# One layer (linear attention and a gated feed-forward) on one core: normalised tiles transposed in pairs, buffers resized, load waits moved, work re-ordered

## The chip, the cores and the metric

The kernel runs on one core of a Trainium2 chip. A core has a matmul engine (TensorE: PE in the profile, its weight loads PEld), a vector engine (VectorE: DVE), a scalar engine (ScalarE: ACT), a general engine (GpSimd: POOL), and a queue engine (SyncE: SP) that issues transfers; each runs its own stream of instructions in order, and they meet by semaphores. The metric is the device time of one execution in microseconds (us), as the median of the runs.

## The reference

Batch 1, 2048 rows, width 448, 16 heads of 28, feed-forward width 1792, all bf16:

```python
qkv = layernorm(x) @ wqkv                                   # q, k, v: 16 heads of 28
pq, pk = q @ w_phi[h], k @ w_phi[h]                         # per head
phi_q = concat(softmax(pq), softmax(-pq))                   # 56 features per head
phi_k = concat(softmax(pk), softmax(-pk))
kv, z = einsum("sf,sd->fd", phi_k, v), sum_s(phi_k)         # over all 2048 rows
o = (phi_q @ kv) / (phi_q @ z + 1e-6)
h = x + o @ wo
h2 = h + (sigmoid(g) * u) @ w_down                          # g, u = layernorm(h) @ w_gate, @ w_up
```

## The kernel before

**Tiles.** The 2048 rows are 16 tiles of 128 (NT). The feed-forward runs in five chunks of 2, 4, 4, 4 and 2 tiles (CH). Width 448 is padded to four blocks of 128 columns in the transposed arrays (the blocks overlap, and a matmul reads only the rows that are its own).

**First the weights.** The q and k weights are transposed (WT, copies WTc at L460/L463), centred, and multiplied by w_phi (fold, copies W2 at L483/L486), so that a projection gives the features' logits at once. v's weights are centred (Wvc).

**Keys.** For each tile: projection of k and v (kp, vp), two exponentials of plus and minus the logits on ACT (L599), a sum per head on DVE (ss, L612), its reciprocal (rs, L615), the scaling phi (L619, on POOL or DVE), and kv (L632), which adds the tile to one running product. When tile 15 is in, kvz (L696, DVE) masks and copies that product; nothing of the attention's output can start before it.

**Queries.** Projections qp, exponentials (eqp, eqm, L654), sums of the halves (hs on POOL, L668; sq on DVE, L671), reciprocals rq (L673, L675), the scaling em (L681, POOL or DVE), and a transpose by DMA into eqT (eT, L689; tiles 0 to 3 one by one, the others in pairs). Scaled features lie in a ring of NEQ buffers. Some scalings on DVE and on POOL are kept from running side by side: each waits for the last one of the other engine in the order (L127 to L134).

**Output of the attention.** num (numerator and denominator, L705), rd and o (division, L713 and L715, into o_pad), the transpose oT (tiles 0 and 1 by matmul and copy, oP L723 and oT L729; the others by DMA in pairs, L736), the output projection (wo_, for tiles 0 and 1 on top of x at L744; for the others a pair of tiles as two matmul streams on the upper and lower 64 rows of the array, `pair` and `half`, L510 to L522). Each pair has two halves of 4 and 3 passes; the second adds to the banks of the first.

**Second normalisation.** h (sum, L769), statistics (L772, L774), rs2 by a power on POOL (ve2 L775, pow2 L777), nb (L788), and hn (L784 for tiles 0 and 1, else L790 on ACT or L792 on DVE) into a ring of NHN buffers. Then the transpose hT into hnT: tiles 0 and 1 by matmul and copy (hP L798, copies L804/L807), tiles 2 to 15 each by one DMA transpose on SP (L810). hnT is the same memory as xT, the transposed input that the projections read.

**Feed-forward.** For each chunk and pair of 128-wide blocks: gate and up products as two 64-row streams (gu, L514 through `half`), tanh on ACT (tg, L845; the sigmoid is (tanh(g/2)+1)/2), hh = (tanh+1)*u on DVE (L852), then per tile the down product (dn, L871), the sum with h on DVE (fin, L878), and the store (st, L880). In the last chunk the down products, copies and stores are split into 336 and 112 columns (a and b), and tile 15's last store is issued by ACT, all others by SP. Dummy matmuls (dm, L814) can be placed where PE would stand still.

**The order.** Every piece of work is a task with a number. PLAN (L30 to L72) is the order of all tasks, written out: the task's number, after a point the banks of PSUM that it takes, and "~" where it runs on its other engine. `emit` (L148) walks the list once, puts each task at the end of its engine's queue, and adds the waits that its inputs, its bank and its buffer need. Loads, transposes and stores have their own rings of semaphores; before one certain store SP waits for the whole ring of loads and transposes (L170 to L175): the store with eight left to go, the eleventh of 18.

Of the kernel before, what the change touches and what calls it, by code (L numbers as in the profile page):

```python
# [10 lines left out]
P = 128  # L11
# [19 lines left out]
8 16 17 11 9 14 43 10 1 0 23 24 25 26 27 28 29 30 31 32 33 34 35 44 36 37 38 39 40 41 42 52 56 50 51 46 3 18 4 19 45  # L31
6 55 47 48 57.7-7 58 59 60 61 661.0-0 70.0-0 71 67.1-1 118 2 15 12 13 64.2-2 73.3-3 68 20 119 65 74 22 72 69 66~ 75
120 21 165.4-4 167.5-5 62 63 662.0-0 91.6-6 92 94.7-7 95 88.0-0 89 97.1-1 98 121 93~ 7 122 123 124 5 90~ 96~ 166 99
168 112.2-2 113 127 125 114 115 128 126 169.3-3 171 173 175 79.4-4 170.6-6 172 174 193.0-1 176 177.5-7 178 194
76.2-2 180 179 182 80 183 116 129 117 130 184 131 186 187 189 136 190 138 134 132 135 137 133 139 191 81 195.3-6 181
188 185.4-4 196 204 197 198 205 206 199 211.5-7 192 229.0-1 212 85.6-6 140 141 142 200 77 78 201 207 86 216 215 87
208 149 202 223 222 82.3-3 230 213.2-5 203 209 218 83 219 220 225 145 226 147 143 146 148 150 144 227 151 152 153 84
214 217 224 234 231.6-7 210 100.3-3 101 232 233 235 103.2-2 104 247.0-5 221 102 240 241 109.6-6 248 105 251 252 236
160 237 238 243 158 244 161 254 255 154 156 159 155 157 245 249.1-3 110 106.2-2 107 228 108 250 111 259 253 242 258
265.0-2 239 266 270 269 319.1-6 320 246 256 162 163 261 262 272 327 328 276 277 322 321 329 273 257 263 283.5-7  # L40
267.0-6 284 164 287 288 274 279 330 280 290 323 281 331 291 324 268 301.1-2 260 302 335.3-5 264 271 295 278 294 305
306 292~ 325 332 326 334 333 663.0-0 285.0-6 336 286 303.1-7 275 312 289 313 338 282 293 304 353.0-2 297 298 299 345
314 337 344 296 307 515.7-7 354 421.3-5 300 362 356 363 355 308 315 309 316 310~ 317~ 311 318 422 455 519.6-6
461.1-1 370.0-2 456.4-4 346 347 339 364 462 348 340 463 457 341 458 349 357 342 350 54 53 49 352 358 365 359 366 343
351 371 464.1-1 459.4-4 423 430 424 465 460 520 521 516 517 537 543 372 431 522 373 380 379 404.1-3 387.5-6 518 388
389 469.4-4 360 367 361 368~ 544 538 369 545 539 470 546 540 405 547.0-0 541.2-2 466.7-7 471 374 381 390 407 548 396
406 542~ 664.5-5 665.5-5 701.4-5 702.0-2 703 704 705 707 413 414 397 467 468 382 375 706 476.1-1 473.7-7 708 477 474
478 475 709.4-5 710.0-2 711 712 717.1-3 718.6-7 719 720 391 398 376 383 713 715 714 723 721 472 479 523.4-5 524 384
377 385 378 392 399 400 393 716 722 725.0-2 726.1-3 727 728 729 549 557 731 550 724 525.4-5 526 551 732 558 559 565
730 573 733.6-7 734.1-3 735 736 394 401 402 395 408 560 552 553 554 561 566 562 386 403 737 738 567 568 741.0-2  # L50
742.4-5 743 744 739 555 563 569 574 740 575 747 570 745 571 748 576 415 746 556 564 438.6-7 749.1-3 750.4-5 751 752
753 755 577 578 754 756 416 439 490.0-0 480.2-2 487.1-1 483.3-3 760.4-4 481 491 492 484 485 482 432 409 761 433 488
434 489 410 579 572 580 763.0-5 764.2-3 765 766 440 448 447 441 769 767 771.6-7 772.1-4 773 774 425 435 449 426 427
417 428 436 411 450 770 418 451 452 442 775 768 777 412~ 443 444 778 776 779.2-3 780.0-5 781 782 785 783 786 486 493
527.1-4 787.6-7 788.0-5 789 790 784 793 791 794 792 529.2-3 528 530 795.0-5 796.6-7 797 798 589 581 597 799 801 598
605 582 583 606 802 800 599 803.1-4 804.2-3 805 806 807 809 811.6-7 812.0-5 813 814 607 590 808 815 817 816 810 818
591 757.1-1 419 762 420 494.4-4 758 495 429 584 437 445 496 497.6-6 504.7-7 505 498 499 453 600 446 608 609 610 601
602 585 454 586 587 588 611 603 822.2-2 823 759 500 592 593 594 511.3-3 595 825.0-0 506 828.5-5 508.1-1 531.4-6
501.2-2 826 512 513 502 829 532 621 613 503 509 510 612 604 596 831.0-7 832.3-5 833 834 835 837 836 614 838 839.4-6
840.1-2 841 842 843 845 847.0-7 848.3-5 849 850 844 853 851 846 615 616 617 618 622 623 619~ 624 625 626 852 854  # L60
855.4-6 856.1-2 857 858 859 861 862 507 514 620 827 860 533.0-7 863.3-5 864.1-2 865 866 867 534 868 627~ 628 869 637
# [6 lines left out]
991.4-7 992.2-6 993 994 999.1-5 1000.0-3 1001 1002 995 997 998 996 1007.2-6 1008.4-7 1009 1010 1005 1003 1004 1006  # L68
1015.1-5 1016.0-3 1017 1018 1011 1012 1013 1019 1021 955.2-2 1022 956 1014 1023.6-6 958.0-0 961.3-3 1031.2-2 1020
962 1035.4-4 1036 1032 1033 959 964.7-7 965 1024 895 889 1034 892 898 957 963 960 966 1025 1026 1027.1-1 1037 1038  # L70
1028 1029 1030
"""  # L72


# [5 lines left out]
class _Graph:  # L80
# [67 lines left out]
    def emit(self, rings):  # L148

        nc = self.nc  # L150
        done = self.planned()
# [769 lines left out]
```

## Time and profile before

| | us |
|---|---|
| median of three runs | 206.84 (206.36, 206.84, 206.85) |
| the profiled execution | 206.24 |
| its span in the profile | 204.5 |

The span is the time from the first to the last event that the profile holds; 1.7 us of the execution lie around it. A row of a view has a start, a length, an engine, a line of the kernel and the operation; "[0.50 <-PE ps L514]" says that the engine stood still for 0.50 us before, and what ended that. The costliest group is the gate and up product, whose two streams are two groups of 490 matmuls each with 87.0 and 86.8 us that overlap each other; next comes the down product with 43.5 us.

### The profile page before, as it was taken

The numbers are of one execution on the slowest core, as the hardware profiler recorded it, in microseconds if no ns is written. First come the engines' busy times: TensorE is split into PE (matmuls) and PEld (weight loads), VectorE is DVE, ScalarE is ACT, GpSimd is POOL, SyncE is SP. The second block draws the span as 40 slices with busy tenths as digits, with TensorE's granted clock in tenths as the row PEclk, the third lists the DMA queues.
The fourth block names the chain that finished last, engine by engine and source line by source line (L and its number), as shares of the span: only waits on it lengthen the run. The fifth ranks groups of instructions, "written<-read, shape, count | busy, mean of one in ns | idle before, by whom it ended". The sixth has DMA issues, their size and how long they took to land.

```text
span 204.5 us, 5003 instructions
## 1 busy us (share of the span) xinstructions
PE 196.8 (96%) x2029; PEld 106.5 (52%) x2029; DVE 132.7 (65%) x306; ACT 96.0 (47%) x182; POOL 79.0 (39%) x141
## 2 busy tenths in 40 slices
PE   7899999999999998999999999999999999999993
PEld 3444454445377764555555544444544444886562
DVE  2999999898799979729574466465128345543033
ACT  3789999998983580423342042423002443551000
POOL 8569999768759865600830003003000300000000
PEclk9999999999999999999999999999999999999999
DMA  5999997059683955191155151013200004000014
GB/s 147 272 268 222 307 383 215 0 110 340 135 132 75 188 88 104 44 168 40 40 114 103 30 103 27 24 27 27 72 0 0 3 11 109 3 3 0 0 42 140
DMA packets 49751, 21.06 MB, mean 103 GB/s; under 512 B 40512, under 2 KB 48704, under 8 KB 49728
## 3 DMA queue, kind: packets, MB, share of 16 engines
q1 hardware_dynamic: 49584, 20.71, 44.6%
q8 instruction: 16, 0.26, 0.5%
q14 instruction: 7, 0.06, 0.1%
q10 hardware_dynamic: 144, 0.03, 0.1%
HBM read 9.20 MB, written 1.84 MB: 54 GB/s over the span
## 4 chain that ended last, share of the span: by engine, by line
PE 76%; ACT 7%; DVE 6%; POOL 5%; issue 2%; DMA 2%; SPq 1%; DVEq 0%; POOLq 0%; ACTq 0%
PE ps L514 51%; PE ps L871 21%; POOL hh L619 3%; ACT eq L654 2%; ACT hh L599 2%; DVE ssum L612 2%; DMA wphK<-in_A_w_phi_dram 2%; PE ps L705 1%; DVE hh L619 1%; POOL rs L543 1%; DVE x_sb L878 1%; PE ps L585 1%; SPq L358 1%; DVE sq L671 1%; PE ps L475 1%
## 5 line engine op out<-in xcount | busy, mean ns | idle before, releaser
L514 PE MATMUL ps<-xT,wg_sb 64*128 64x512 bf16 (+1 forms) x490 | 87.0, 333 | 1.1 <-DVE x_sb L878 0.7
L514 PE MATMUL ps<-xT,wu_sb 64*128 64x512 bf16 (+1 forms) x490 | 86.8, 333 | 0.0
L845 ACT ACTIVATE tg<-ps 128x512 f32<-128x512 f32 (+1 forms) x70 | 33.9, 511 | 76.8 <-PE ps L514 76.1
L852 DVE SCALAR_TENSOR_TENSOR hh<-tg,ps 128x512 bf16<-128x512 f32 (+1 forms) x70 | 38.2, 573 | 32.1 <-ACT tg L845 31.9
L514 PEld LDWEIGHTS ps<-xT,wg_sb 64*128 64x128 bf16 x490 | 45.6, 94 | 22.7 <-issue 1.9
L514 PEld LDWEIGHTS ps<-xT,wu_sb 64*128 64x128 bf16 x490 | 45.6, 94 | 15.2
L871 PE MATMUL ps<-wd_sb,hh 128*128 128x448 bf16 (+2 forms) x252 | 43.5, 332 | 0.0
L871 PEld LDWEIGHTS ps<-wd_sb,hh 128*128 128x128 bf16 x252 | 22.9, 98 | 19.3 <-issue 1.0
L878 DVE SCALAR_TENSOR_TENSOR x_sb<-ps,x_sb 128x448 bf16<-128x448 f32 (+2 forms) x18 | 10.0, 566 | 24.4 <-PE ps L871 24.4
L775 POOL TENSOR_SCALAR rs<-mv 128x1 f32<-128x1 f32 x14 | 2.7, 192 | 59.7 <-DVE mv L774 58.8
L619 POOL TENSOR_TENSOR hh<-hh,rsum 128x896 bf16<-128x896 bf16 x13 | 21.9, 1700 | 0.5 <-DVE rsum L615 0.5
L599 ACT ACTIVATE hh<-ps,rs 128x448 bf16<-128x448 f32 x32 | 18.7, 643 | 2.0 <-PE ps L585 1.1
L654 ACT ACTIVATE eq<-ps,rs 128x448 bf16<-128x448 f32 x32 | 18.1, 649 | 0.0
L612 DVE TENSOR_REDUCE ssum<-hh 128x32 f32<-128x896 bf16 x16 | 16.9, 1058 | 0.8 <-ACT hh L599 0.6
L668 POOL TENSOR_TENSOR halves<-eq 128x448 f32<-128x448 bf16 x14 | 13.4, 970 | 8.3 <-DVE sq L671 2.7
L514 PE MATMUL ps<-Wvc,xT 64*128 64x448 bf16 x112 | 13.2, 351 | 0.2
L681 POOL TENSOR_TENSOR eq<-eq,rq 128x448 bf16<-128x448 bf16 x14 | 13.0, 942 | 1.0 <-DVE eq L681 0.8
L514 PE MATMUL ps<-Wq,xT 64*128 64x448 bf16 x112 | 13.1, 351 | 0.1
L514 PE MATMUL ps<-Wk,xT 64*128 64x448 bf16 x98 | 11.5, 351 | 0.2
L514 PE MATMUL ps<-wo_sb,oT 64*128 64x448 bf16 x98 | 11.3, 350 | 0.1
L790 ACT ACTIVATE hn<-x_sb,nb,rs 128x512 bf16<-128x512 bf16 x10 | 7.8, 810 | 5.5 <-POOL nb L788 3.0
L715 DVE TENSOR_TENSOR o_pad<-ps,rden 128x448 bf16<-128x448 f32 x16 | 9.8, 620 | 0.2
(104 smaller groups left out, 186.4 us busy)
## 6 DMA issues: line engine op xcount, KB each, us to landing
wu_sb<-in_B_w_up_dram SPq DMA_DIRECT2D x2, 896.0 KB, 8.2
wg_sb<-in_B_w_gate_dram SPq DMA_DIRECT2D x2, 896.0 KB, 7.5
out_dram<-x_sb SPq DMA_DIRECT2D x14, 112.0 KB, 1.8
x_sb<-in_A_x_dram SPq DMA_DIRECT2D x3, 448.0 KB, 4.1
wd_sb<-in_B_w_down_dram SPq DMA_DIRECT2D x3, 448.0 KB, 4.6
hh<-in_A_wqkv_dram SPq DMA_DIRECT2D x4, 196.0 KB, 3.6
wo_sb<-in_A_wo_dram SPq DMA_DIRECT2D x2, 336.0 KB, 9.5
x_sb<-in_A_x_dram SPq DMA_DIRECT2D x2, 224.0 KB, 4.0
```

The source lines that it names most:

```text
L514: r = e.matmul(ap(), lhsT=st(blk, rows), rhs=mv(blk, rows), start=first and i == 0, stop=not first and i == 2, tile_position=(rows.start, 0))
L599: task((key, t), "act", 0.53, lambda e, t=t, s=s, i=i, b=kb: e.activation(signs(ek[:, s, :])[:, :, :, i, :], heads2(bank[b()][:, 0:D]), AC ...
L612: task(("ss", t), "dve", 1.0, lambda e, s=s: e.tensor_reduce(ssum[:, s, :], ek[:, s, :].rearrange("p (h d) -> p h d", d=DH), AX.X, ALU.add ...
L619: return e.tensor_tensor(phi[:, t % NPHI, :, 0:GP].rearrange("p k (a d) -> p k a d", d=DH), ek[:, s, :].rearrange("p (k a d) -> p k a d", ...
L654: task((key, t), "act", 0.53, lambda e, w=w, t=t, i=i, b=bk[j]: e.activation(signs4(eq[:, w, :, 0:GP])[:, :, :, i, :], heads2(bank[b()][:, ...
L668: task(("hs", t), "pool", 0.9, lambda e, w=w, half_=half_, by4=by4: e.tensor_tensor(half_, by4(eq[:, w, :, 0:GP])[:, :, :, 0:DH // 2], by4 ...
L681: return e.tensor_tensor(ap, ap, rq[:, w, :].rearrange("p (k h) -> p k h", h=2)[:, :, :, None].to_broadcast([P, NPAIR, 2, DH]), ALU.mult)
L715: task(("o", t), "dve", 0.56, lambda e, t=t, res=res: e.tensor_tensor(o_pad[:, t % 4, 64 * (t % 2):64 * (t % 2) + D].rearrange("p (h d) -> ...
L845: task(("tg", c, f_), "act", 0.51 if n == 4 else 0.3, lambda e, j=j, N=N, b=gb[i]: e.activation(tg[:, j % NSG, 0:N], bank[b()][:, 0:N], AC ...
L852: e.scalar_tensor_tensor(hhT[c % 2][:, f_, 0:N], tg[:, j % NSG, 0:N], 1.0, bank[b()][:, 0:N], op0=ALU.add, op1=ALU.mult), deps)
L871: r = e.matmul(bank[b][:, cols], lhsT=hhT[c % 2][:, f_, ts], rhs=wd_sb[:, f_, cols], start=(f_ == 0), stop=(f_ == FT - 1))
L878: e.scalar_tensor_tensor(X(t)[:, cols], bank[got(first)[0]][:, cols], 0.5, X(t)[:, cols], op0=ALU.mult, op1=ALU.add), [nm, ("hn", t)])
```

## The change

1. hnT is laid out tile by tile, `[p, tile, block, column]` where it was `[p, block, row]`, in the same memory. Tiles 2 to 15 are transposed in pairs: 7 DMA transposes of two tiles each, with a destination that is one stretch for the pair, where 14 single ones were. A pair waits for both normalised tiles, and for the projections of the input tiles over whose memory it writes: tile t lies over the columns of one block of input tiles 4(t mod 4) to 4(t mod 4)+3, for tiles 0 to 15 alike.
2. The gate and up products read their moving operand as `hnT[rows, t0:t0+n, blk, :]`: n runs of 128 columns, where it was one run of 128n.
3. NEQ is 12 (14), NHN is 4 (3).
4. SP's waits for the rings of loads and transposes stand before the first store that follows the issue of the last transpose (the ninth store in the new order).
5. PLAN is another order. On PE, seen from the order of each engine: the keys' projections of tile pair 0 have their halves next to each other; before the first gate product the query projections of pairs 3 to 6 stand earlier, among tile 0's and tile 1's output work; the output projections of tiles 2 and 3 and of 4 and 5 have their halves parted by the halves of query projection 7; three dummies where five stood; the last down products run in another order and the last one is tile 15's. On the other engines: tile 12's phi is POOL's (DVE's before); em.0, em.4 and em.5 are DVE's (em.5 and em.10 before), em.0 ahead of kvz; h.0, hn.5, hn.6 and hn.8 are DVE's (ACT's before), hn.11, hn.12 and hn.14 ACT's (DVE's before); one weight copy (WTc.1.0) is ACT's (DVE's before). On SP the weight loads of the feed-forward all stand ahead of the first feature transpose, and the last store is ACT's, of tile 15's narrow columns.

```diff
-    NEK, NPHI, NV, NEQ, NSG, NHN = 3, 3, 3, 14, 3, 3
+    NEK, NPHI, NV, NEQ, NSG, NHN = 3, 3, 3, 12, 3, 4
...
-        hnT = xT
+        hnT = xT[:].rearrange("p k s -> p (k s)").rearrange("p (t k s) -> p t k s", t=NT, k=4)
...
-            n_out = sum(t.kind == "out" for t in done)
+            n_tr, checked = sum(t.kind == "tr" for t in done), False
             for t in done:
-                if t.kind == "out" and nring.get("out", 0) == n_out - 8:
+                if t.kind == "out" and nring["in"] == rings["in"] and nring["tr"] == n_tr and not checked:
+                    checked = True
                     for k in ("in", "tr"):
                         for j in range(min(nring[k], rings[k])):
                             wait("sp", ring_sems[k][j], (k, j), 16 * ((nring[k] - 1 - j) // rings[k] + 1))
...
+        HT = {t: ("hT", t if t < 2 else t - t % 2) for t in range(NT)}
...
-            free = [opt(("hT", t - NHN))]
+            free = [opt(HT.get(t - NHN))]
...
-            read = [Q_OF[t], ("kp", t // 2, 1), ("vp", t // 2, 1)]
+            over = [4 * (i % 4) + j for i in ((t,) if t < 2 else (t - 1, t)) for j in (0, 2)]
+            read = [d for i in over for d in (Q_OF[i], ("kp", i // 2, 1), ("vp", i // 2, 1))]
...
-            else:
-                task(("hT", t), "sp", 1.25, lambda e, t=t: e.dma_start_transpose(
-                    out=hnT[:, :, TS(t)], in_=hn[:, t % NHN, :]), [("hn", t)] + read, lat=1.6 if t < 6 else 2.8, kind="tr", size=0.72)
+            elif t % 2:
+                task(("hT", t - 1), "sp", 1.25, lambda e, t=t: e.dma_start_transpose(
+                    out=hnT[:, t - 1:t + 1, :, :].rearrange("p t k s -> p (t k) s"),
+                    in_=hn[:, (t - 1) % NHN:(t - 1) % NHN + 2, :].rearrange("p t k -> p (t k)")),
+                    [("hn", t - 1), ("hn", t)] + read, lat=1.6 if t < 6 else 2.8, kind="tr", size=1.42)
...
-                    return (lambda: bank[b()][:, 0:N], lambda blk, rows: w[rows, blk, fs], lambda blk, rows: hnT[rows, blk, cs])
+                    return (lambda: bank[b()][:, 0:N], lambda blk, rows: w[rows, blk, fs], lambda blk, rows: hnT[rows, t0:t0 + n, blk, :])
...
-                             [nm + (i, 0)] if h else GU_W + [("hT", t) for t in range(t0, t0 + n)],
+                             [nm + (i, 0)] if h else GU_W + [HT[t] for t in range(t0, t0 + n)],
```

The copies of tiles 0 and 1 (L804, L807) write `hnT[:, t, :, :]` in place of `hnT[:, :, TS(t)]`. The numbers in PLAN are left out here: task numbers shift by the seven transposes that are gone, so its text differs throughout.

More of the change, by code (lines that the diff above doesn't have):

```diff
@@ L36 @@
[L36 to L45, printed above, removed]
@@ new lines @@
+932.0-2 933.3-7 934 935 938 936 937 939 940.1-6 941.4-5 942 943 944 946 945 947 960.0-2 961.3-7 962 963 968.1-6
+969.4-5 970 971 964 966 967 965 972 974 975 973 976.3-7 977.0-2 978 979 980 982 981 983 984.4-5 985.1-6 986 987 988
+990 991 989 992.3-7 993.0-2 994 995 1008.1-6 1009.4-5 1010 1011 998 996 997 999 1012 1013 1000.3-7 1001.0-2 1002
+1003 1006 1007 954.1-1 948.6-6 951.0-0 952 1004 949 1005 955 957.2-2 1016.0-0 958 1024.6-6 950 953 814 959 1014 1015
+1020.3-3 1021 1022 1023 888 1017 1018 1019 956 1025 1028.7-7 1026 1027 1029 1030 1031
```

74 lines of the change are left out of this document (38 added, 36 removed).

## The prediction

> **What bounds the kernel now.** First the head of the profile's page, then busy time by stage (columns: window, its length, busy time and instruction count of PE, PEld, DVE, ACT, POOL, then PEclk, DMA share, GB/s).
>
> ```profile
> span 204.5 us, 5003 instructions
> PE 196.8 (96%) x2029; PEld 106.5 (52%) x2029; DVE 132.7 (65%) x306; ACT 96.0 (47%) x182; POOL 79.0 (39%) x141
> ```
> ```profile
> 0.00:10.00 10.00, 7.57 (x55) 3.98 (x55) 5.97 (x25) 5.23 (x9) 7.21 (x26) 1.00 0.86 210
> 10.00:47.00 37.00, 36.43 (x430) 17.48 (x431) 34.97 (x76) 35.17 (x67) 30.23 (x32) 1.00 0.82 215
> 47.00:58.00 11.00, 10.24 (x109) 4.77 (x111) 9.61 (x27) 10.17 (x21) 9.28 (x15) 1.00 0.88 236
> 58.00:78.54 20.54, 19.68 (x301) 13.98 (x302) 18.34 (x49) 11.87 (x26) 14.31 (x27) 1.00 0.67 108
> 78.54:201.41 122.87, 122.86 (x1140) 66.25 (x1140) 63.50 (x131) 33.58 (x62) 17.99 (x44) 1.00 0.23 47
> 201.41:204.50 3.09, 0.00 (x0) 0.00 (x0) 0.30 (x2) 0.00 (x0) 0.00 (x0) 1.00 0.51 158
> ```
>
> TensorE's clock is granted in full everywhere, so no term below is a clock's. From 78.54 to 201.41 PE is busy 122.86 of 122.87 us: there only fewer or cheaper matmuls help, and the matmuls stay the same in number and size. From 10 to 58 DVE and ACT are nearly as full as PE, so the first 58 us are a balance of four engines in which PE's time is stretched by whichever is late. What is left is the gap before 78.54 (20.54 less 19.68 in that stage) and the 3.09 us after the last matmul. The chain of waits (start, length, what) names the joints:
>
> ```profile
> 57.98 1.71 PE ps L514 x28
> ...
> 75.20 2.67 PE ps L871 x14
> ...
> 78.54 23.98 PE ps L514 x224
> ...
> 185.33 15.39 PE ps L871 x98
> ...
> 200.75 0.69 DVE x_sb L878 x2
> 201.44 0.27 DVE x_sb L878
> ```
>
> The first gate product starts at 57.98 (G below), the second chunk's at 78.54, and the end is a copy and a store behind the last down product.
>
> **The change, part by part.**
>
> *Front, up to G.* The new order gives tile 12's K scaling to POOL, one weight copy to ACT, and em.0, em.4 and em.5 to DVE (before: em.5 alone of these). h.0 moves to DVE too, behind ve2.0, where it runs while POOL takes tile 0's power: 0. Rows of the timeline:
>
> ```profile
> 35.78 3.36 POOL L619 TENSOR_TENSOR hh<-hh,rsum 128x896 bf16<-128x896 bf16 x2
> ...
> 40.80 1.84 POOL L681 TENSOR_TENSOR eq<-eq,rq 128x448 bf16<-128x448 bf16 x2
> 42.60 1.70 POOL L619 TENSOR_TENSOR hh<-hh,rsum 128x896 bf16<-128x896 bf16 x1
> ```
> ```profile
> 39.45 1.09 DVE L619 TENSOR_TENSOR hh<-hh,rsum 128x896 bf16<-128x896 bf16 x1 [0.22 <-POOL rq L675]
> ...
> 44.43 2.09 DVE L619 TENSOR_TENSOR hh<-hh,rsum 128x896 bf16<-128x896 bf16 x2
> 47.02 0.64 DVE L696 TENSOR_TENSOR kvz<-ps,maskP 112x464 bf16<-112x464 f32 x1 [0.49 <-PE ps L632]
> ...
> 53.87 0.62 DVE L681 TENSOR_TENSOR eq<-eq,rq 128x448 bf16<-128x448 bf16 x1 [0.16 <-POOL eq L681]
> ...
> 55.55 0.26 DVE L713 RECIPROCAL rden<-ps 128x16 f32<-128x16 f32 x1 [0.93 <-PE ps L705]
> ```
>
> POOL is free of tile 11 at 39.13. From there it runs two small rq (0.2 each; DVE's 0.22 of waiting at 39.45 was for one), scaling 12 (1.70), one em (0.92) and scaling 13 (1.70): 43.8. DVE's sums come 1.09 earlier without scaling 12, so its last two scalings (2.09) start at 43.8 and end at 45.9 instead of 46.53: kvz could start 0.63 sooner. em.0 (0.62) now stands on DVE ahead of kvz, in a place where DVE waits 0.49 for PE: +0.13. em.4 and em.5 are both on DVE between the two tiles' statistics and their normalising, one more than before: +0.62, unless it falls into DVE's 0.93 us wait at 55.55. Tile 0's features are scaled last (45.9 + 0.62 = 46.5, where POOL had them at 42.6), so its numerator comes behind tile 1's by the length of a transpose, and four more projection parts are ordered ahead of it; these parts are work that PE did later before, so they cost G only as far as tile 0 waits for them. A freer DVE in the start stage gives perhaps 0.3. Sum: -0.63 + 0.13 + 0.62 - 0.3 = **-0.2**. Bounds: -1.4 (the extra em falls into the wait of 0.93 and tile 0 is not late, -0.8; and POOL, lighter by 0.92 for each em given away, brings tile 0's last scale another 0.6 forward) and +1.2 (no gain at the start, 0.62 in full, tile 0 later by its own 0.62 and 0.4 more). Two of five dummies go:
>
> ```profile
> L814 PE MATMUL ps<-warm 128*128 128x512 bf16 x5 | 2.0, 429 | 0.0
> ```
>
> They stand where PE has nothing to do, so 0; if that cover were gone they'd be worth at most 2 x 0.2 (each starts 0.2 behind the last, judged by the 512-column row below).
>
> *Output projection pairs of tiles 2 to 5.* The two halves of a pair stood next to each other; now a query projection's half or the next pair's half stands between. The window of one pair back to back (14 matmuls, 7 passes of two streams) and of a stretch with foreign work between the halves (20 matmuls, 10 passes), tile wo_sb, and the weight load that waits:
>
> ```profile
> 63.54:65.10 1.56, 1.48 (x14) 1.00 0.63 117
> 91.57:93.46 1.89, 1.88 (x20) 1.00 0.80 180
> ```
> ```profile
> 64.34 0.30 PEld L514 LDWEIGHTS ps<-wo_sb,oT 64*128 64x128 bf16 x6 [0.50 <-PE ps L514]
> ```
>
> 1.56 / 7 = 0.223 us a pass against 1.89 / 10 = 0.189: 7 x 0.034 = 0.24 for each pair, the second half waiting for the first to leave the array. Two pairs: **-0.47** (0 to -0.5).
>
> *The wait before the second chunk.* The waits of PE put it at DVE's copy L878, but that copy isn't an input of the product; its other condition is the landing of tile 5's transpose. Waits, timeline, the group of the same operation on DVE, and the transposes (us to landing):
>
> ```profile
> PE ps L514 <- DVE x_sb L878: 0.7, 1, 0.7
> ```
> ```profile
> 72.35 0.97 POOL L668 TENSOR_TENSOR halves<-eq 128x448 f32<-128x448 bf16 x1
> ...
> 74.25 0.81 ACT L790 ACTIVATE hn<-x_sb,nb,rs 128x512 bf16<-128x512 bf16 x1 [0.20 <-POOL nb L788]
> ```
> ```profile
> L792 DVE TENSOR_SCALAR hn<-x_sb,rs,nb 128x512 bf16<-128x512 bf16 x4 | 1.6, 409 | 0.6 <-POOL nb L788 0.6
> ```
> ```profile
> xT<-hn SPq DMA_TRANSPOSE x14, 2.4
> ...
> oT<-o_pad SPq DMA_TRANSPOSE x7, 3.1
> ```
>
> Tile 5 is normalised at 75.06 on ACT; its transpose makes the product start at 78.54, 3.48 later. In the new order POOL's 0.97 us no longer stands ahead of tile 5's POOL chain and DVE takes 0.41 for 0.81: normalised at 75.06 - 0.97 - 0.40 = 73.7. A pair's transpose has the size of the o_pad ones, 3.1 against 2.4: 73.7 + 3.48 + 0.7 gives 77.9, and 73.7 + 3.1 alone 76.8. PE, 0.47 earlier, ends the down product at 77.87 - 0.47 = 77.4. I take the o_pad row, since queue and DMA load fall with half as many transposes: the wait goes, **-0.6** (the 0.69 less some queueing). At 77.9 it would leave 0.5. Bounds -0.69 and +0.8: the pair's transpose must wait for both tiles and, in the tile-by-tile layout, for the projections of tiles 8 to 15; if one of these is behind, the wait grows by the 1.5 us its transposed tile is then late less the 0.7 gained. The Trainium skill, "DMA: Bandwidth & Descriptors", section "Latency and other measured facts", gives a DMA transpose 261 GB/s with a non-contiguous middle dimension and 350 to 400 when contiguous. By it a pair of 256 KB now written contiguously would take an estimated 0.7 us for its bytes against 1.0 for two singles, and the sum would be lower by at most 0.1, since the wait is already gone; the rows here (2.4 and 3.1) show mostly fixed time.
>
> *Tail.* SP's 18 waits for loads and transposes, the queue of the last nine stores, and the landing of the two kinds of last store:
>
> ```profile
> L166 SPq EVENT_SEMAPHORE  x18: 27/28/28, 198.5 to 199.5; - x18
> ```
> ```profile
> 197.64 5.27 SPq L880 DMA_DIRECT2D out_dram<-x_sb  x9
> ```
> ```profile
> out_dram<-x_sb ACTq DMA_DIRECT2D x1, 28.0 KB, 1.6
> out_dram<-x_sb SPq DMA_DIRECT2D x1, 28.0 KB, 1.5
> ```
>
> Before, the last copy ends at 201.71, but SP's queue runs until 202.91: nine issues of some 0.42 and about 1.1 of waits in one piece. After, the waits stand before the ninth store, which is issued as soon as the last transpose is out and SP has time, and the very last store is ACT's, whose queue is empty. End = last matmul + 0.30 (copies) + 0.05 + 1.6 (landing) + 0.5 (from landing to the end of the span: 204.50 - 202.49 - 1.5) = 2.45 for 3.09: **-0.65** (-0.7 to -0.2, where SP's own last store still ends later). Behind the moved waits stand nine stores and nothing else, so nobody waits for them.
>
> *New read layout.* Gate and up products now read four or two runs of 128 columns, not one run of 512 or 256. Windows of the same matmuls, source L514:
>
> ```profile
> 153.50:174.65 21.15, 21.15 (x200) 9.61 (x198) 1.00 0.12 31
> 174.65:185.35 10.70, 10.68 (x196) 9.27 (x192) 1.00 0.01 2
> ```
>
> 200 records stand for 2 x 98 passes: 0.2158 us a pass of 512, 0.1092 of 256. Halving the columns costs 2 x 0.1092 - 0.2158 = 2.6 ns for the extra start. If each run cost a start: 3 x 2.6 ns x 294 passes + 2.6 ns x 196 = **+2.8** at most; I take 0, as a run is one stride in one instruction and not a new instruction. The Trainium skill, "SBUF — State Buffer", section "Specifications (TRN2)", has lines of 16 bytes with a penalty for each step to a new line unless it is hit twice; by it a run of 128 bf16 is 16 whole lines, and the sum stays as it is.
>
> *The rest at 0.* Twelve feature buffers for fourteen, four normalised buffers for three, half as many transposes on SP, and weight loads ahead of the first feature transposes: all hidden behind PE, which is never short after 78.54. If that cover failed, a late transpose would cost what the wait above did, 0.7.
>
> Sum: -0.2 - 0.47 - 0.6 - 0.65 = -1.92. The profiled execution took 206.24 (1.73 more than its span), the median of the runs is 206.84; -1.92 gives 204.3 for such an execution and **204.9** for the median.
>
> **Rivals.** (1) The front gains more: every early scaling counts and tile 0 isn't late, -1.2 instead of -0.2: 203.9. For it: DVE and ACT are 95% busy from 10 to 47, so each relief counts. Against: tile 0 is scaled last. (2) The pair's transpose is late and the second chunk waits as before, or some more: -1.92 + 0.6 + 0.4 = 205.9. For it: one transfer now waits for two tiles. (3) The front order loses what the rest gains: +1.2 for -0.2, with the wait half kept (+0.3): 206.6; the change then does little. For it: DVE gets two more em. Against: its 0.93 us of waiting. (4) Slower: PE pays a start for each run of 128 columns, +2.8 on a PE that has no slack: 204.9 + 2.8 = 207.7. There are 294 x 3 + 196 = 1078 more runs; it outweighs the gains of 1.92 from 1.8 ns a run, and shows as slower from 2.4. For it: the only rows that bear on it show a cost per start. Against: these starts were whole instructions.
>
> **How the numbers follow.** Forecast 0.48, rival (1) 0.14, (2) 0.14, (3) 0.13, (4) 0.11. No change means within 0.3%, 206.2 to 207.5, about what a measurement of this kernel can tell. (4) and a little beyond it is slower: 0.11; (3) is the same, 0.13; faster 0.76. The range holds forecast, (1), (2) and most of (3): 203.5 to 206.8.
>
> **What would show it.** In the profile after: the stage behind the last matmul 2.4 to 2.5 us and ACT's store last; no wait of 0.7 before the second chunk's first gate product; pass times of 0.2158 and 0.1092 as now; the first gate product 0 to 1 us earlier; the last scaling on DVE ending near 45.9. Wrong would make it: passes of 0.22 or more, a new wait of PE behind a pair's transpose in a later chunk, or tile 0's copy later than 57.98.

## The result and the profile after

| | before | after |
|---|---|---|
| median of 20 runs | 206.82 us | 205.56 us |
| lowest and highest | 206.36, 207.42 | 205.19, 206.85 |
| first profiled execution, its span | 206.24, 204.5 | 206.85, 205.0 |
| a second profiled execution, its span | | 205.28, 203.5 |

The ratio of the times is 0.9951 (95% interval 0.9937 to 0.9964): the change is faster by 0.5%, 1.0 us. (The medians lie 1.26 us apart; the ratio goes by the means, which the slowest runs of the changed kernel pull up.) 205.56 lies in the range given, 0.66 above the 204.9 forecast. The 20 runs of the changed kernel are not one heap: 14 lie between 205.2 and 205.7, two near 206.1, and four between 206.67 and 206.85. The first profile caught the upper heap; for the comparison with before the second one, from the lower heap, is used. Busy time by stage of the second execution, cut at the same joints as before (columns as in the prediction: window, its length, busy time and count of PE, PEld, DVE, ACT, POOL, then PEclk, DMA share, GB/s):

```profile
0.00:10.00 10.00, 7.72 (x55) 4.39 (x56) 5.61 (x24) 5.69 (x10) 6.82 (x26) 1.00 0.87 209
10.00:47.00 37.00, 36.04 (x432) 17.92 (x433) 35.40 (x78) 34.91 (x66) 30.75 (x32) 1.00 0.90 251
47.00:58.06 11.06, 10.21 (x106) 4.54 (x103) 10.30 (x29) 10.12 (x20) 8.47 (x14) 1.00 0.62 117
58.06:78.34 20.28, 19.62 (x300) 14.26 (x301) 18.34 (x51) 10.64 (x25) 15.56 (x28) 1.00 0.72 107
78.34:201.21 122.87, 122.86 (x1140) 66.17 (x1140) 62.47 (x128) 34.78 (x63) 17.60 (x44) 1.00 0.23 49
201.21:203.50 2.29, 0.00 (x1) 0.00 (x0) 0.28 (x1) 0.00 (x0) 0.00 (x0) 1.00 0.35 106
```

The same view of the first execution:

```profile
47.00:59.51 12.51, 11.44 (x127) 5.40 (x126) 11.75 (x31) 11.57 (x23) 8.63 (x14) 1.00 0.56 105
59.51:79.84 20.33, 19.62 (x300) 14.27 (x301) 18.38 (x51) 10.65 (x25) 15.61 (x28) 1.00 0.75 107
79.84:202.71 122.87, 122.87 (x1140) 66.07 (x1140) 62.39 (x128) 34.76 (x63) 17.55 (x44) 1.00 0.23 49
202.71:205.00 2.29, 0.00 (x0) 0.00 (x0) 0.27 (x1) 0.00 (x0) 0.00 (x0) 1.00 0.34 106
```

Three of the four stages are alike in both executions: the one up to the second chunk takes 20.3 us, the long middle 122.87, the tail 2.29. Only the first gate product differs, 58.06 against 59.51. So these two executions, one from each heap, part ahead of it.

Term by term, the profile of before against the second one of after (us, one execution each):

| stage | before | after | moved | forecast |
|---|---|---|---|---|
| up to the first gate product | 57.98 | 58.06 | +0.1 | -0.2 |
| from there to the second chunk | 20.56 | 20.28 | -0.3 | -1.07 |
| middle | 122.87 | 122.87 | 0 | 0 |
| behind the last matmul | 3.09 | 2.29 | -0.8 | -0.65 |
| span | 204.5 | 203.5 | -1.0 | -1.92 |

The waits of PE (engine, line, waited for: total, times, longest) in the second execution, those behind the first gate product, and the end of its timeline:

```profile
PE ps L514 <- DMA xT<-hn: 0.4, 1, 0.4
...
PE ps L874 <- DVE hh L855: 0.3, 1, 0.3
```
```profile
201.25 0.28 DVE L881 SCALAR_TENSOR_TENSOR x_sb<-ps,x_sb 128x112 bf16<-128x112 f32 x1 [0.18 <-PE ps L874]
201.56 0.37 ACTq L883 DMA_DIRECT2D out_dram<-x_sb  x1
```

Of the 0.69 us of waiting before the second chunk 0.4 is still there, now under its true name, and a wait of 0.3 for DVE that was not there before stands ahead of the down product. The last store is ACT's, right behind the last copy. The passes of the gate and up products, 200 and 196 records as before:

```profile
153.30:174.45 21.15, 21.15 (x200) 9.59 (x198) 1.00 0.12 30
174.45:185.13 10.68, 10.68 (x196) 9.28 (x192) 1.00 0.01 3
```

21.15 and 10.68 us for 98 passes each, where it was 21.15 and 10.70: reading four or two runs of 128 columns costs nothing.

### The profile page after: what moved, and what is told of

Read it like the earlier page. It is cut to its first block, busy times and chain, and to the rows that moved or that the text cites. A ratio compares the mean times of both kernels' runs of the same rounds, so it can differ in the third digit from the quotient of the medians.

```text
span 205.0 us, 4981 instructions
## 1 busy us (share of the span) xinstructions
PE 198.1 (97%) x2026; PEld 108.4 (53%) x2027; DVE 132.5 (65%) x306; ACT 96.3 (47%) x182; POOL 79.2 (39%) x141
## 4 chain that ended last, share of the span: by engine, by line
PE 79%; POOL 7%; DVE 5%; ACT 4%; DMA 2%; issue 1%
PE ps L514 51%; PE ps L874 20%; POOL halves L668 3%; DMA xT<-hn 2%; PE ps L632 2%; POOL eq L681 2%; ACT hh L460 1%; POOL rs L778 1%; PE ps L475 1%; PE ps L426 1%; DVE o_pad L715 1%; PE ps L585 1%; ACT hh L599 1%; ACT hh L604 1%; ACT eq L654 1%
## 5 line engine op out<-in xcount | busy, mean ns | idle before, releaser
L848 ACT ACTIVATE tg<-ps 128x512 f32<-128x512 f32 (+1 forms) x70 | 34.5, 510 | 84.5 <-PE ps L514 63.6
L619 POOL TENSOR_TENSOR hh<-hh,rsum 128x896 bf16<-128x896 bf16 x14 | 23.6, 1698 | 1.3 <-DVE rsum L615 1.1
L599 ACT ACTIVATE hh<-ps,rs 128x448 bf16<-128x448 f32 x32 | 18.6, 647 | 2.3 <-PE ps L514 1.9
L681 POOL TENSOR_TENSOR eq<-eq,rq 128x448 bf16<-128x448 bf16 x13 | 12.0, 938 | 0.3
L514 PE MATMUL ps<-wo_sb,oT 64*128 64x448 bf16 x98 | 10.4, 349 | 0.0
L604 ACT ACTIVATE hh<-ps,rs 128x448 bf16<-128x448 f32 x16 | 10.3, 654 | 0.1
L770 DVE TENSOR_TENSOR x_sb<-ps,x_sb 128x448 bf16<-128x448 f32 x14 | 8.1, 617 | 3.2 <-PE ps L514 3.2
## 6 DMA issues: line engine op xcount, KB each, us to landing
wd_sb<-in_B_w_down_dram SPq DMA_DIRECT2D x3, 448.0 KB, 10.2
```

The lines of the kernel that those rows point to most:

```text
L514: r = e.matmul(ap(), lhsT=st(blk, rows), rhs=mv(blk, rows), start=first and i == 0, stop=not first and i == 2, tile_position=(rows.start, 0))
L599: task((key, t), "act", 0.53, lambda e, t=t, s=s, i=i, b=kb: e.activation(signs(ek[:, s, :])[:, :, :, i, :], heads2(bank[b()][:, 0:D]), AC ...
L604: return e.activation(v1[:, t % NV, :, 0:DH], bank[b()][:, 0:D].rearrange("p (h d) -> p h d", d=DH), ACT.Copy, scale=rs1[:, 0, t:t + 1])
L619: return e.tensor_tensor(phi[:, t % NPHI, :, 0:GP].rearrange("p k (a d) -> p k a d", d=DH), ek[:, s, :].rearrange("p (k a d) -> p k a d", ...
L681: return e.tensor_tensor(ap, ap, rq[:, w, :].rearrange("p (k h) -> p k h", h=2)[:, :, :, None].to_broadcast([P, NPAIR, 2, DH]), ALU.mult)
L848: task(("tg", c, f_), "act", 0.51 if n == 4 else 0.3, lambda e, j=j, N=N, b=gb[i]: e.activation(tg[:, j % NSG, 0:N], bank[b()][:, 0:N], AC ...
```

## The experiments

Each kernel ran beside the kernel before on the same chip; a ratio is to that, with its 95% interval. The changed kernel itself stands at 0.9946 to 0.9951. The runs from the singles to the halves together were made on another chip than the first four and the last; the changed kernel itself did not run there, so they are held against it by the stages of their profiles.

### The changed kernel again

No edit.

> The changed kernel as it is, to see a second execution of it. Its first profile (206.85) shows matmuls at half rate until 10.6 us (weight transposes 0.38 apart), where the kernel before has them at full rate from 5.2 us; its runs lie in two heaps, around 205.5 and around 206.8. Theory A (the start decides the heap): an execution near 205.5 shows full-rate matmuls from about 5 to 6 us on, and its first gate product about 1.2 us earlier than 59.51; one near 206.8 shows them late again. Rival B (the heap is decided later, by the landing of the paired transposes): the first gate product stands at 59.5 in both, and the second chunk's start moves by 1.2. Median 205.4 to 206.0.

Measured: 205.47 median of six runs, 205.28 to 205.56; ratio 0.9946 (0.9930 to 0.9963). Theory A holds for the place: the profile is of the lower heap, and its first gate product stands at 58.06, 1.45 before the other's. The row of the column sums (L491: duration min, median, max of the matmul, first and last start), second and first execution:

```profile
L491 PE MATMUL ps<-hh,ones x3: 350/352/354, 7.9 to 8.4; 128*128 128x448 bf16 x3
```
```profile
L491 PE MATMUL ps<-hh,ones x3: 581/581/581, 8.8 to 10.0; 128*128 128x448 bf16 x3
```

The same matmul takes 352 ns in one execution and 581 in the other, while the PEclk of both first windows reads 1.00. That reading says nothing of this stretch: the clock records in the traces begin, with 1.00, only at 6.06 us in the second execution and at 10.52 in the first (5.00 in the profile of before), and time without a record is printed as full. These are the moments from which matmuls follow one another at twice the rate. Over all fourteen profiles of this case the rate doubles between 4.5 and 7.3 us in ten, among them all four with the front order of before, and between 9.4 and 10.9 in the other four.

### One dummy given back in the start

```diff
 xP.1
+dm.3
 fold.1.2.0
```

> The changed kernel with one dummy matmul given back in the start, behind tile 1's transpose product, where PE stands still for 0.6 us. Theory A (PE gets its full rate late when the start has a gap, and the dropped dummy was what filled it): the heap near 206.8 becomes rare or goes, median 205.2 to 205.6. Rival B: both heaps stay in the same shares (about 5 of 20 near 206.8), the median moves by less than 0.2.

Measured: 205.55 median of six (205.19 to 205.78), ratio 0.9948 (0.9932 to 0.9964). No run of the upper heap, but the changed kernel as it is had none on this chip either. The run doesn't tell the theories apart.

### The waits alone

The kernel before with the new condition for the waits.

```diff
-                if t.kind == "out" and nring.get("out", 0) == n_out - 8:
+                if t.kind == "out" and nring["in"] == rings["in"] and nring["tr"] == n_tr and not checked:
```

> The kernel before with the waits for loads and transposes at the new place and nothing else. Tail theory (18 waits of about 1.1 us stand between SP's last nine stores, and SP's queue ends 1.2 us behind the last copy): -0.4 to -0.6, the stage behind the last matmul 2.5 us instead of 3.09. Rival (the landing of the last store sets the end, and the stores' issues pile up whatever the waits do): within 0.15.

Measured: 205.76 median of eight against 206.57, ratio 0.9964 (0.9949 to 0.9978), -0.7 us, a little more than expected. The stage behind the last matmul in its profile:

```profile
201.92:204.30 2.38, 0.00 (x0) 0.00 (x0) 0.31 (x2) 0.00 (x0) 0.00 (x0) 1.00 0.38 109
```

2.38 for 3.09. This one condition gives some 70% of what the whole change gains (0.36% of 0.49 to 0.54%); the new order of the last products, which makes ACT's store the last one, adds 0.1 at most (2.29).

### The halves parted alone

The kernel before, order on PE:

```diff
-gu.0.4.1.1 wo_.1.0 wo_.1.1 gu.0.6.0.0 gu.0.6.1.0 gu.0.6.0.1 gu.0.6.1.1 wo_.2.0 wo_.2.1
+wo_.1.0 gu.0.4.1.1 wo_.1.1 gu.0.6.0.0 gu.0.6.1.0 gu.0.6.0.1 wo_.2.0 gu.0.6.1.1 wo_.2.1
```

> The kernel before with the halves of the output projections of tiles 2, 3 and of 4, 5 parted by a half of the gate and up product that stood ahead of them, and nothing else. Each pair alone saves 0.24 us of PE. If PE sets the time there: -0.47 up to the second chunk's down product, and as long as that chunk waits for tile 5's transpose, -0.2 to -0.47 in all, since tile 5's statistics come earlier as well. Rival (the wait for the transpose takes it all): 0, with a wait of 1.1 us before the second chunk's first gate product.

Measured: 207.66 against 206.57, ratio 1.0053 (1.0036 to 1.0070): slower by 1.1, which neither side expected. The waits of DVE between 62 and 72 us, before and here:

```profile
DVE hh L852 <- ACT tg L845: 0.3, 1, 0.3
```
```profile
DVE hh L851 <- ACT tg L844: 1.7, 2, 0.9
```

A half of gate and up was put off by one projection half (0.76), ACT's tanh came later, and DVE, which runs in order, stood 1.4 us longer at the products hh; the sums of tiles 4 and 5 stand behind those in its queue and start some 1.3 us later (69.51 and 70.34 for 68.22 and 69.09). PE's waits between 60 and 82 us add up to 1.8 for 0.7, which is the 1.1 lost. The experiment parted the halves with the wrong work, so it says nothing of the price of 0.24; the last but one below does it with the work that the change uses.

### Tiles 2 to 5 one by one

```diff
-HT = {t: ("hT", t if t < 2 else t - t % 2) for t in range(NT)}
+HT = {t: ("hT", t if t < 6 else t - t % 2) for t in range(NT)}
...
+            elif t < 6:
+                task(("hT", t), "sp", 1.25, lambda e, t=t: e.dma_start_transpose(
+                    out=hnT[:, t, :, :], in_=hn[:, t % NHN, :]), [("hn", t)] + read, lat=1.6, kind="tr", size=0.72)
             elif t % 2:
```

> The changed kernel with tiles 2 to 5 transposed one by one (in the tile-by-tile layout, four DMA transposes for two), the other tiles in pairs. In the second profile of the changed kernel tile 5 is normalised at 73.90, its pair lands at 78.21, and the second chunk's first product starts 0.4 after the down product before it ended (78.00). Theory P (a pair takes 1.2 to 1.9 us longer to land here than a single did in the kernel before, and this keeps the wait): a single for tile 5 lands near 77, the wait goes, -0.3 to -0.45 against the changed kernel, 205.1. Rival (the place is slow, whatever the size: several transposes queue there): four singles land no sooner than the two pairs, 0 to +0.4.

Measured: 206.95 median of twelve against 206.54, ratio 1.0024 (1.0005 to 1.0042). Theory P falls: the wait of PE did not go, it grew. That wait, and the issues of the four transposes with their time to landing:

```profile
PE ps L514 <- DMA xT<-hn: 1.6, 1, 1.6
```
```profile
L812 SPq DMA_TRANSPOSE xT<-hn x4: 1190/1214/2414, 72.4 to 77.5; - x4
...
DMA to landing us min/median/max: 2.4/3.1/4.3
```

PE waits 1.6 us for the four singles where it waited 0.4 for the two pairs: one of them takes 4.3 us to land, the issue of the next holds SP for 2.4, and the last is issued only at 77.5, 3 us after its tile was there. (Its first gate product is at 58.54, half a microsecond later than in the changed kernel, which is the rest of the loss.) Something holds transposes up at this place whatever their size, and two of them suffer less from it than four.

### The pairs alone

The kernel before in its order, with the new layout, pairs and NHN 4 (NEQ 14).

```diff
+    NEK, NPHI, NV, NEQ, NSG, NHN = 3, 3, 3, 14, 3, 4
...
-hT.2 hT.3 hT.4 hT.5
+hT.2 hT.4
```

> The kernel before, in its own order, with the tile-by-tile layout, the paired transposes and four normalised buffers, and nothing else of the change (14 feature buffers, the old waits). Each pair stands where its later tile is normalised. Theory P: the second chunk's wait grows by what a pair takes longer, +0.7 to +1.2: 207.3 to 207.9. The prediction's view (fewer transposes relieve the queue): -0.6 to 0. Read layout: the passes of 512 columns stay at 0.2158 us; a cost for each run of 128 columns would show as up to 0.2236.

Measured: 207.47 median of eleven against 206.54, ratio 1.0044 (1.0030 to 1.0059), +0.9. PE's wait before the second chunk is 1.6 us for 0.7. The size is theory P's, the cause is another, as SP's waits between 66 and 80 us show:

```profile
SPq L165 <- PE ps L514: 4.2, 1, 4.2
```

SP waits 4.2 us for PE before it issues the pair of tiles 2 and 3: in the order of before query projection 7 ends at 74.2, and the pair writes over the transposed input of tiles 8 to 15, which that projection reads. In the new order this projection stands between the halves of the output projections, some 7 us sooner. Parting the halves is thus not the only use of that move: with the projection in its old place the pairs cost 0.9 instead of helping.

### Fewer dummies

The changed kernel with NWARM 3 for 5 and without the first dummy.

> The changed kernel without its dummy in the start and with three warm-up matmuls for five; no other work is touched, and PE stands still in their place, waiting for the first weights. Theory A (PE comes to full rate only behind a stretch in which it was kept busy): matmuls at half rate until 8 us or later in most executions, +0.6 to +1.3 against the changed kernel, near the heap of 206.8. Rival (the dummies are idle filling and the late heap is the loads'): within 0.2.

Measured: 207.07 median of twelve (206.12 to 207.61), ratio 1.0018 (1.0002 to 1.0034). Its profiled execution has the column sums at 353 to 577 ns, the rate doubling in the midst of them:

```profile
L491 PE MATMUL ps<-hh,ones x3: 353/477/577, 8.7 to 9.6; 128*128 128x448 bf16 x3
```

Its first gate product is at 58.90. That agrees with theory A, but the chip of this run (shared by the runs from the singles to the halves together) showed late starts with all dummies as well, 577 ns in both profiles of the lengthened stream, so it is no proof that the dummies are the cause.

### Tile 0's query scaling back on POOL

```diff
-phi.12 em.1 phi.13 rq.0
+phi.12 em.1 rq.0 em.0 phi.13
```

> The changed kernel with tile 0's query scaling back on POOL, ahead of the scaling of tile 13's keys, as in the kernel before. Prediction's front term: em.0 leaves DVE (-0.62 ahead of kvz) but tile 13's scaling, and with it DVE's last two, come 0.9 later: kvz +0.3, tile 0's numerator 2 to 3 us sooner. If the chain from kvz through both tiles sets the first gate product: +0.1 to +0.4. Rival (tile 0's lateness ate the front's gain: its output o.0 is 1.7 later than in the kernel before): the first gate product comes 0.3 to 0.8 sooner.

Measured: 207.75 median of six, ratio 1.0053 (1.0034 to 1.0072), 1.1 slower than the kernel before; its profiled execution is 2.3 slower than the changed kernel's (207.59 for 205.28). POOL's timeline there, then in the changed kernel:

```profile
42.45 0.94 POOL L681 TENSOR_TENSOR eq<-eq,rq 128x448 bf16<-128x448 bf16 x1
43.35 1.70 POOL L619 TENSOR_TENSOR hh<-hh,rsum 128x896 bf16<-128x896 bf16 x1
```
```profile
42.05 1.70 POOL L619 TENSOR_TENSOR hh<-hh,rsum 128x896 bf16<-128x896 bf16 x1
```

Tile 13's keys are scaled until 45.05, and in the changed kernel until 43.75; kvz (47.8 for 46.7) and the first gate product (59.18 for 58.06) follow by 1.1. So a later kvz reaches the first gate product in full, and POOL's em.0 ahead of tile 13's keys is dear: taking it away from POOL was right. Tile 0's lateness does not show as a cost of its own: tile 0 is scaled sooner here, and the first gate product still follows kvz. It does not follow that an earlier kvz gains as much; the front's term, further down, comes back to this. The other 1.1 us arises behind it: the second chunk starts 21.38 us after the first gate product for 20.28, because the pair of tiles 4 and 5 lands 5.2 us after its issue for 4.1, as the critical chain has it:

```profile
75.22 5.20 DMA xT<-hn
```

### PE's stream made longer

Seven (and in the second run four) fulfilled waits behind each half of the first chunk's gate and up products.

```diff
+                    if t.eng == "pe" and t.name[:2] == ("gu", 0):
+                        for _ in range(7):
+                            queues["pe"].append(lambda e, w=latest["pe"]: e.wait_ge(*w))
```

> The changed kernel with 196 more instructions in PE's stream: after each half of the first chunk's gate and up products seven waits that are already fulfilled; no work is added or moved. Theory C (PE's instructions come in blocks of 16 KB by DMA; one block's transfer, at 75.5 in the second profile, runs while the paired transposes of tiles 2 to 5 are under way, and they stand still until it is done): the block that came at 75.5 now comes behind the first product of the second chunk; the pair of tiles 4 and 5 lands 3.1 to 3.3 us after its issue instead of 4.1, the wait of 0.4 before the second chunk goes, -0.3 to -0.45 against the changed kernel, near 205.1. Rival (a paired transpose is slow at this place for another cause): landing 4.1 to 4.5 after issue as before; the time is the same or up to 0.3 more for the waits.

> The same with four waits for seven, 112 instructions. Theory C: the block that came at 75.5 comes about 3 us sooner, at 72 to 73, and now meets the transposes of tiles 6 to 9's query features or the first pair; the pair of tiles 4 and 5 lands in 3.1 to 3.5 us, but the features may come 1 us later and hold the numerators of tiles 6 to 9: -0.4 to +0.6 against the changed kernel. Rival: as in the run with 196.

Measured: 207.69 median of twelve, ratio 1.0017 (0.9986 to 1.0048), with seven; 205.92, 0.9954 (0.9922 to 0.9986), with four. As a cure both miss: the block didn't move as far as reckoned (75.8 and 76.4 us, in executions whose starts were late by 1.5), and with four the pairs at the second chunk still take 4.1 and 4.7. As a test of what holds a transpose up they speak clearly. First the DMA view of the changed kernel from the issue of the pair of tiles 2 and 3 to the second chunk: GB/s in 40 slices of 0.14 us, and the packets that are instructions:

```profile
GB/s 0 0 0 0 0 0 0 0 40 199 217 221 208 203 205 201 167 132 61 192 331 219 171 59 23 5 2 7 11 9 11 9 165 287 296 143 0 0 0 0
...
q8 instruction: 1, 0.02, 1.0%
...
xT<-hn SPq DMA_TRANSPOSE x2, 4.5
```
```profile
DMA to landing us min/median/max: 4.1/4.5/4.9
```

For about 1.1 us in the middle (8 slices) the transposes move 2 to 23 GB/s, where they move some 200 before; then the rest follows at once. One packet of kind instruction lies in the window of this view; in the trace it runs from 75.48 to 76.41, so it begins half a microsecond ahead of the gap, and the gap (76.0 to 77.2) outlasts it. The two pairs take 4.9 and 4.1. The next pairs of the same kernel (tiles 6 to 9) have none and no such gap, and land in 3.2:

```profile
GB/s 0 0 0 0 0 0 0 0 0 0 11 130 214 225 207 212 216 214 198 184 203 189 124 107 200 221 209 216 203 214 216 209 200 198 130 12 0 0 0 0
...
xT<-hn SPq DMA_TRANSPOSE x2, 3.2
```

With four more waits behind each half of the first chunk, 40 us earlier, and no other edit, the same two pairs:

```profile
GB/s 0 0 0 0 0 0 0 0 42 316 207 208 181 79 9 0 0 0 9 7 9 11 9 90 282 293 268 276 260 216 230 212 196 197 200 53 4 0 0 0
...
q8 instruction: 1, 0.02, 1.4%
...
xT<-hn SPq DMA_TRANSPOSE x2, 4.3
```

The gap and the packet have come to them, and they land in 4.3. With seven waits the pair of tiles 4 and 5 is free of the block and lands 3.1 after its issue (3.9 for the pair before it), as theory C has it:

```profile
L817 SPq DMA_TRANSPOSE xT<-hn x2: 1250/1892/2533, 75.2 to 77.9; - x2
...
DMA to landing us min/median/max: 3.1/3.5/3.9
```

But it is issued only at 77.9, since the issue of the pair before it holds SP for 2.5 us, and another block meets the o_pad transposes of tiles 2 and 3 (4.6 us to landing for 3.3). The second chunk starts 21.5 us after the first gate product (81.08 less 59.56) for 20.3, and that is mostly PE's own time:

```profile
59.56:81.08 21.52, 21.18 (x300) 13.84 (x301) 18.37 (x51) 10.88 (x25) 15.32 (x28) 1.00 0.75 101
```

PE is busy for 21.18 us there, with the same matmuls that took 19.62; with four waits it is 19.74. So seven waits behind each half were not free: PE itself comes 1.2 us later to the second chunk, so neither the time of this run nor the fact that PE no longer waits for the transposes tells what the block costs. Theory C holds for the landings; the blocks only move on to other transposes. That the packets are PE's instructions is inferred: the page has 16 of them with 0.26 MB, and only PE's stream was touched.

```profile
q8 instruction: 16, 0.26, 0.5%
```

### The halves together again

```diff
-wo_.1.0 qp.7.0 wo_.1.1 wo_.2.0 qp.7.1 wo_.2.1
+wo_.1.0 wo_.1.1 qp.7.0 wo_.2.0 wo_.2.1 qp.7.1
```

> The changed kernel with the halves of the output projections of tiles 2, 3 and of 4, 5 next to each other again (query projection 7 in two parts behind them). PE works 0.47 longer up to the second chunk. In the second profile of the changed kernel the down product before that chunk waits 0.3 for a product of DVE (the one behind tile 5's normalising) and the chunk itself 0.4 for the transposes. Theory W (those two waits hide the gain): within 0.15 of the changed kernel. Rival (the prediction's term): +0.4 to +0.5.

Measured: 207.06 median of twelve, ratio 1.0025 (0.9998 to 1.0052). Its profiled execution (206.11, with an early start) is to be held against 205.28: +0.8, more than either. ACT's longest wait between 60 and 80 us, here and in the changed kernel:

```profile
ACT eq L654 <- PE ps L514: 3.8, 1, 3.8
```
```profile
ACT eq L654 <- PE ps L514: 2.7, 1, 2.7
```

The same matmuls of the output projections and of query projection 7 up to the next gate product, in the changed kernel and here (rows of PE's timeline):

```profile
63.59 0.92 PE L514 MATMUL ps<-wo_sb,oT 64*128 64x448 bf16 x8
...
67.56 0.27 PE L514 MATMUL ps<-xT,wg_sb 64*128 64x256 bf16 x1
```
```profile
63.61 1.73 PE L514 MATMUL ps<-wo_sb,oT 64*128 64x448 bf16 x14
...
68.06 0.27 PE L514 MATMUL ps<-xT,wg_sb 64*128 64x256 bf16 x1
```

They take 3.97 us parted and 4.45 together: 0.48, the prediction's 0.47. The second half of query projection 7 is now last. ACT's exponential of it stands ahead of two tanh in ACT's order, so ACT waits 1.1 longer, DVE's products come 1.1 later, and tile 5's statistics with them. So this run moved two things, the parting and the place of the projection's last half, which ends 1.06 us later (68.06 for 67.00): 0.48 of that is the price of the halves, the rest is the place. The time cannot be put down to the parting alone.

### The start filled

The changed kernel with two dummies behind xP.1 and one behind csum.

> The changed kernel with three more dummies in the start: two behind tile 1's transpose product, where PE stands still for 0.6 to 0.8 us, and one behind the column sums. Seen so far: matmuls turn to full rate between 4.5 and 7.3 us in nine profiles, and only behind 8.6 us in four (the two with 206.85 and 206.21 for the changed kernel with all and with fewer dummies, and both with the shifted code). Theory A (the rate is raised only at the end of a stretch of some 3.4 us in which PE was kept busy, and the gap before the first fold product spoils such a stretch in part of the executions): with the gap filled no profile and no run is of the late kind, all runs lie within 205.1 to 205.9. Rival (the late kind comes from elsewhere, the loads or the chip): some of the runs lie above 206.4 again.

Measured: 205.64 median of six (205.28 to 205.87), ratio 0.9943 (0.9926 to 0.9960). No late run, and none faster. On the chip where the changed kernel showed no late run either, this decides nothing; what makes a start late stays open beyond its place.

## Why the prediction was right, and where it was not

**Direction and bound.** Right: the middle did not move (122.87), the read layout is free, and rival (4), the only slower one, is out. But the forecast gain was too large, 1.92 us where the two profiles show 1.0 and the medians 1.26. The result is nearest to rival (2), 205.9, which had the pair's transpose late, and the range held because it took that rival in.

**Tail, -0.65.** Right, with 0.8 measured; undersized by 0.15. The kernel before with the waits alone, -0.7, shows that it is mainly the waits that did it.

**The wait before the second chunk, -0.6.** Here the prediction failed, in two of its steps. Tile 5 was normalised at 73.89, close to the 73.7 forecast. But "3.1 alone gives 76.8": the pairs take 4.1 and 4.9 us at this place, where a block of instructions comes by DMA in all fourteen profiles, and the product started at 78.34. The trace of before had it: of its 14 singles, the one that took 4.3 is tile 4's, at this place, and tile 5's behind it took 3.2.

```profile
DMA to landing us min/median/max: 2.4/2.4/4.3
```

The median over the kernel was taken for the price of this place. And "DVE takes 0.41 for 0.81" left out what is queued behind tile 5's normalising on DVE. The timeline of the second execution:

```profile
73.48 0.41 DVE L793 TENSOR_SCALAR hn<-x_sb,rs,nb 128x512 bf16<-128x512 bf16 x1
73.80 1.30 DVE L855 SCALAR_TENSOR_TENSOR hh<-tg,ps 128x256 bf16<-128x256 f32 x3
```

The last three products of the first chunk stand behind it until 75.1, and the down product that needs them waits 0.3. PE ended that down product at 77.99, where 77.4 was forecast.

**The pairs' halves, -0.47.** The price was right: the same matmuls take 0.48 less when parted (the run with the halves together). It did not reach the end. PE's busy time in this stage sank by no more than 0.06, from 19.68 to 19.62, so PE lost some 0.4 again at other places of the new order, which no run takes apart, and the wait of 0.3 came on top. The chunk itself waited for tile 5's transpose, which landed later still; a saving on PE there is worth nothing until that comes earlier. In the sum the two terms were added as if each stood alone.

**Front, -0.2.** Measured +0.1, within its bounds, but not the way that was forecast. The chain did come earlier, by less than reckoned:

```profile
44.06 2.09 DVE L619 TENSOR_TENSOR hh<-hh,rsum 128x896 bf16<-128x896 bf16 x2
...
46.65 0.64 DVE L696 TENSOR_TENSOR kvz<-ps,maskP 112x464 bf16<-112x464 f32 x1
47.84 0.62 DVE L671 TENSOR_REDUCE sq<-halves 128x32 f32<-128x448 f32 x1 [0.54 <-POOL halves L668]
```

The last scaling ends at 46.15 (46.52 before, 45.9 forecast) and kvz starts 0.4 sooner, where 0.5 was reckoned. Right behind kvz DVE then stands 0.54 us for POOL's halves, which wait for ACT's exponentials; before, DVE went on at once, at 47.67. From there to the first gate product it takes 10.2 us, and 10.3 before. The step that failed is that kvz was taken for the one limit of this stage: the critical chain of the changed kernel comes to the first gate product by the exponentials and the halves (POOL, 46.84 to 50.78), so an earlier kvz gains nothing alone, while a later one costs in full, as the run with em.0 on POOL shows. The sign does not hang on one execution: four profiles with the front order of before have the first gate product at 57.75 to 58.12, five with the new one and an early start at 58.06 to 58.54.

**Dummies, 0, and "no term below is a clock's".** Wrong in the second part. PEclk reads 1.00 throughout, yet matmuls at the start run at half rate until 4.5 to 10.9 us, and which it is decides some 1.3 us of the execution. In the eleven traces that have a clock record it lasts 194.56, 197.97 or 201.39 us, steps of 3.41 apart, and the late records (from 10.52 and 10.90) begin one such step behind 7.11 and 7.49. The Trainium skill, "TensorE: Matmul & The Clock Gate", section "Part 1: The HAM clock gate (the "warmup" mystery)", has such a half rate that ends after a busy window of some 3.4 us, in windows that run free of the kernel's start; the steps of 3.41 agree. By that a gap in PE's work in the start can spoil a window. Whether the dropped dummy matters for it is not shown. The traces fit it: without a dummy in the gap before the first fold product (some 6.2 to 7.0 us) the records begin by 6.28 or else a step late, and with one there they could begin at 6.95 and 7.27 (the waits alone, one dummy given back).

## What to carry to other kernels

A saving on one engine is not yet a saving at the end: look for what is queued behind the moved instruction on its own engine, on ACT and DVE as on PE, before adding savings up. Two savings ahead of the same wait don't add; the later of the two arrivals is what counts. When the runs of a kernel fall into heaps, profile it again before explaining a difference, and compare stage lengths first: they show in one look where the heaps part. For the price of a transfer take the row of the place, not the median over the kernel.

## What the hardware showed unexpectedly

A transfer of instructions (one packet of 16 KB) held up DMA transposes of pairs for about 1.1 us where it fell among them: 4.1 to 4.9 us to landing for 3.1 to 3.2, at the second chunk in the changed kernel and, with PE's stream lengthened, at the third as well. Counted over all fourteen traces, the paired transposes of hn and o_pad with no such packet near them, 101 of them, landed in 3.0 to 3.3 us; the 22 where one began between 0.7 and 3 us after their issue took 4.1 to 5.2. Where it began at the issue of an o_pad pair or up to 0.6 us behind it, the landing was 3.0 to 3.6 and the issue longer instead. The Trainium skill, "Advanced Engine Details and Errata", section "ISA Cache", gives the instruction cache lines of 16 KB, 256 instructions; 16 packets with 0.26 MB agree with that size.

The rate of the first matmuls (352 or 581 ns for the same instruction) is not seen in the granted clock that the profile prints, because its record begins only where the rate doubles; it is seen in the durations of equal instructions.
